# Global loads moved ahead of the global exchange in the written order of transfers

## The chip, the cores and the metric

The kernel runs on one core of one Trainium2 chip. Time is the device time of one execution in microseconds (us). Engines are named as in the profile: PE is TensorE, DVE VectorE, ACT ScalarE, POOL GpSimd, SP SyncE; SPq is the instruction queue of SP, from which nearly all transfers are issued.

## The reference

For 8 batches of 8 heads, sequences of 512 local and 32 global tokens with 64 elements a head: local tokens attend to the 32 global keys and to a band of 32 keys to either side; global tokens attend to everything. The result, as 4608 rows of 512, goes through a feed-forward network (FFN) with a leaky activation.

```python
s_g = scale * np.matmul(q_g, k_all.transpose(0, 1, 3, 2))
out_g = np.matmul(sm(s_g), v_all)
s_ll = np.where(mask, scale * np.matmul(q_l, k_l.transpose(0, 1, 3, 2)), -1000000000.0)
s_l = np.concatenate([s_lg, s_ll], axis=-1)
out_l = np.matmul(sm(s_l), np.concatenate([v_g, v_l], axis=2))
...
h = x @ w_in
g = np.maximum(h, 0.0) + alpha * np.minimum(h, 0.0)
return (g @ w_out).astype(np.float32)
```

## The kernel before

**FFN steps.** The FFN works on nine groups of tokens (eight batches of 512 local tokens, one of the 256 global tokens), each over 16 blocks of 128 hidden units: 144 steps. Step t computes the hidden block (`f1`, 12 matmuls into `h_ps`), lets ACT, DVE and POOL bend and split it (`g`, `gh`, `gl`), and two steps later adds it to the output (`f2`, 12 matmuls into `o0` to `o3`). One step of 512 tokens is some 5.5 us of matmuls.

**Attention between them.** The attention of later batches is put between the FFN steps. Local work goes by pairs of heads, 32 of them (`P`), one pair every four steps; such four steps are called a round here. Its transfers:

- `load_v` (two transfers, `vw`) and `load_qk` (one, `qk`) bring values, and queries with keys. From the fifth pair on each has a single buffer in SBUF, so the load for the next pair comes after the matmuls of this one.
- `local_scores` (`s_ps` from `qk`) and softmax; then `local_exchange` turns the weights round: DVE transposes 32 by 32 blocks (`pb`), two transfers write them to DRAM, eight read them back in another order (`pt`).
- `local_values` (`o_ps` from `vw` and `pt`), and `local_weights` with an exchange of the result: one transfer out (`xb`), four back (`x_raw`).

Global work goes by two pairs at a time, 16 tasks (`k`), three in every four rounds. `load_gn` brings queries and keys (two transfers, `gn`), `load_vg` values (two, `vg`); `global_scores` computes `g_ps` and its softmax, which ACT writes beside the keys; `global_transposes` is the global exchange: DVE transposes (`sgb`), one transfer out, four back into `sgt_sb`; `global_values` (`go` from `vg` and `sgt_sb`) and `global_outputs` follow with the next task's step. `gn` has one buffer, so task k+1's keys come after task k's scores. `vg` takes two buffers of a ring of three.

**Order.** The start, up to step 18, follows a list of words written by hand (`ORDER`); the word G0 is `global_scores(0)`. After it, a table `at` holds what attention work is done in which step and at which of its places (`pre`, `mid` after `f1`, `post` after the first half of `f2`); `plan` appends to it. Matmuls and the transfers issued by SP stay in the written order; the order on ACT and DVE in that part is the planner's, with a head start for attention work.

Local work of pair P is at step u = 4 (P - 4): values and the next pair's scores with their exchanges at u `post`, `load_v` and `load_qk` at u + 1 `post`. Global tasks stand between, at the steps u of the list `step` (18, 22, 26, 34, ...): scores at u `mid`, exchange at u + 1 `mid`. So in the written order of transfers a round with a global task reads `xb`, `x_raw` x4, `pb` x2, `pt` x8, `vw` x2, `qk`, `sgb`, `sgt_sb` x4, `vg` x2, `gn` x2. At the first step after each batch's end the four stores of results (`out` from `ost`) stand behind `qk`.

SP takes its queue in order: a transfer that waits for its data holds all behind it.

Of the kernel before, what the change touches and what calls it, by code (L numbers as in the profile page):

```python
# [17 lines left out]
NB, NH, SL, SG, D = 8, 8, 512, 32, 64  # L18
# [4 lines left out]
NPR = NB * NPAIR  # L23
# [61 lines left out]
def longformer_ffn(ctx: ExitStack, tc: tile.TileContext, qk, vs, gn, vg, w, alpha, out):  # L85
# [24 lines left out]
    def matmul(*a, **k):  # L110
        return tc.keep_in_program_order(nc.tensor.matmul(*a, **k))  # L111
# [4 lines left out]
    def stage(name, dtype=F32):  # L116
        return work.tile([128, 512], dtype, tag="st", name=name, bufs=NST)

    def small(name, n=4):
        return work.tile([128, n], F32, tag=name, name=name, bufs=4)  # L120
# [7 lines left out]
    def bank(tag, name):  # L128
        return psum.tile([128, 512], F32, tag=tag, name=name, bufs=2 if tag in "hs" else 1)
# [24 lines left out]
    def keep_warm(ps, n, add=False):  # L154
        for _ in range(n):
            matmul(ps, idle[:, 0:128], idle, start=not add, stop=not add)
# [3 lines left out]
    def wide(name, dtype=F32):  # L160
        return work.tile([128, 1024], dtype, tag="dec", name=name, bufs=3)
# [102 lines left out]
    def local_exps(P, heads=(0, 1)):  # L264
        if 0 in heads:
            z_of[P] = small("z", 8)
        for h in heads:
            src, mn, scale = ps_of.pop((P, h))
            p = pr_of[P, h] = stage("p") if P < NRAW else pr_of[P, h]
            for i in range(4):  # L270
                k = 2 * i + h
                act.activation(p[:, 128 * i : 128 * i + 128], src[:, i], AF.Exp, bias=mn[:, i : i + 1], scale=scale, accum_out=z_of[P][:, k : k + 1])
        if 1 in heads:
            rz_of[P] = small("rz", 8)
            act.activation(rz_of[P], z_of.pop(P), AF.Copy, bias=1e-9)
# [14 lines left out]
    def give(src, name):  # L290
        blk = stage(name)
        vec.transpose(blk.rearrange("k (b c n) -> k c b n", b=4, c=4), src.rearrange("q (c b n) -> q c b n", c=4, b=4))
        spread = dram.tile([128, 4, 128], F32, tag=name, name=name, bufs=2)
        dma.dma_start(spread, blk.rearrange("k (b n) -> k b n", b=4))
        return spread

    def take(put, spread):
        for b in range(4):
            dma.dma_start(put[32 * b : 32 * b + 32].rearrange("k (w n) -> k w n", w=4), spread[:, b].rearrange("(w k) n -> k w n", w=4))

    def local_exchange(P, heads=(0, 1)):
        dma.on = True
        for h in heads:
            ps_of[P, h] = give(pr_of.pop((P, h)), "pb")
        if 1 in heads:
            for h in range(2):
                pt_of[P, h] = stage("pt")
                take(pt_of[P, h], ps_of.pop((P, h)))
# [52 lines left out]
    def load_gn(k):  # L361
        if not big:
            big.append(wpool.tile([128, 2048], F32, tag="w", name="gn"))
        for e in range(2):
            gns[2 * k + e] = big[0][:, 576 * e : 576 * e + 576]
            dma.dma_start(gns[2 * k + e], gn[2 * k + e])

    def load_vg(k):
        for P in (2 * k, 2 * k + 1):
            vgs[P] = wide("vg")[:, 0:640].rearrange("k (y d) -> k y d", y=5)  # L370
            dma.dma_start(vgs[P], vg[P])
# [6 lines left out]
    def global_scores(k):  # L378
        ss = gps.pop(k)
        for r, c0, n in ((0, 32, 288), (1, 320, 256)):  # L380
            for e in range(2):
                t = gns[2 * k + e]
                for h in range(2):
                    hs, q0 = slice(64 * h, 64 * h + 64), 64 * r + 32 * e
                    matmul(ss[h][q0 : q0 + 32, 0:n], t[hs, 0:32], t[hs, c0 : c0 + n], start=True, stop=True)
        for e in range(2):
            del gns[2 * k + e]
        m, z = small("gm", 4), small("gz", 16)
        sg_sb = sgs[k] = big[0][:, 1152:1728].rearrange("q (h n) -> q h n", h=2)
        for h in range(2):  # L390
            vec.tensor_reduce(m[:, h : h + 1], ss[h][:, 0:288], axis=AX.X, op=ALU.max)
        vec.tensor_scalar(m[:, 2:4], m[:, 0:2], -0.125, None, op0=ALU.mult)
        vec.tensor_copy(m[0:64, 0:2], m[64:128, 2:4])
        vec.tensor_tensor(m[0:64, 2:4], m[0:64, 2:4], m[0:64, 0:2], op=ALU.min)
        vec.tensor_copy(m[64:128, 2:4], m[0:64, 2:4])
        for h in range(2):
            act.activation(sg_sb[:, h], ss[h][:, 0:288], AF.Exp, bias=m[:, 2 + h : 3 + h], scale=0.125, accum_out=z[:, h : h + 1])
        vec.tensor_copy(z[0:64, 2:4], z[64:128, 0:2])
        vec.scalar_tensor_tensor(z[0:64, 2:4], z[0:64, 2:4], 1e-9, z[0:64, 0:2], op0=ALU.add, op1=ALU.add)
        vec.reciprocal(z[0:64, 2:4], z[0:64, 2:4])  # L400
        vec.tensor_copy(z[64:128, 2:3], z[0:64, 3:4])
        gz[k] = z
# [79 lines left out]
    def f2(T, part, warm=0):  # L482
        G, f = divmod(T, NF)
        kind, b = GROUPS[G]
        n = SL if kind == "l" else NB * SG
        if f == 0 and part == 0:
            obs[G] = [bank(f"o{m}", f"o{m}") for m in range(NC)]
        o = obs[G]
        if T == NT - 1:
            if part:  # L490
                last(T)
            return
        g2 = (gh_of, gl_of)[part][T]
        keep_warm(o[0], warm, f > 0 or part > 0)
        for m in range(NC):
            ms = slice(128 * m, 128 * m + 128)
            if part == 0:
                matmul(o[m][:, 0:n], wts[f, 1][:, 0, ms], g2[:, 0:n], start=(f == 0), stop=False)
                matmul(o[m][:, 0:n], wts[f, 1][:, 1, ms], g2[:, 0:n], start=False, stop=False)
            else:  # L500
                matmul(o[m][:, 0:n], wts[f, 1][:, 0, ms], g2[:, 0:n], start=False, stop=(f == NF - 1))
        if part == 0:
            return
        del gh_of[T], gl_of[T]
        if f == NF - 1:
            col = b * SL if kind == "l" else NB * SL
            for m in range(NC):
                st = stage("ost")
                copy("ad"[m % 2], st[:, 0:n], o[m][:, 0:n])
                dma.dma_start(out[m, :, col : col + n], st[:, 0:n])  # L510

    def last(T):
        G, f = divmod(T, NF)
        n, o = width(T), obs[G]
        for m in range(NC):
            ms = slice(128 * m, 128 * m + 128)
            for j, g2 in ((0, gh_of), (1, gh_of), (0, gl_of)):
                matmul(o[m][:, 0:n], wts[f, 1][:, j, ms], g2[T][:, 0:n], start=False, stop=(g2 is gl_of))
            st = stage("ost")
            copy("ad"[m % 2], st[:, 0:n], o[m][:, 0:n])  # L520
            (dma, act)[m % 2].dma_start(out[m, :, NB * SL : NB * SL + n], st[:, 0:n])
# [3 lines left out]
    def plan(t, where, fn, P):  # L525
        at.setdefault((t, where), []).append((fn, P))
# [13 lines left out]
    for P in range(NRAW + 1, NPR):  # L540
        u = 4 * (P - NPAIR)
# [7 lines left out]
    for k in range(NPR // 2):  # L549
        u, v = step[k], step[k + 1]  # L550
        if k:
            plan(u - 1, "post", global_fill, k)
            plan(u, "mid", global_scores, k)
        plan(u + 1, "mid", global_transposes, k)
        plan(u + 1, "mid", load_vg, k)
        if k + 1 < NPR // 2:
            plan(u + 1, "mid", load_gn, k + 1)
        at.setdefault((v, "mid"), []).insert(0, (global_values, k))
        at.setdefault((v + 1, "mid"), []).insert(0, (global_outputs, k))

# [43 lines left out]
    def first_join(f):  # L604
        join(f)
        if f + 6 < NF:
            load_weights(f + 6)

    on_tensor = {"S": first_scores, "T": local_transposes, "V": first_values, "X": local_outputs, "F": first_f1, "A": lambda T, n: f2(T, 0, n), "B": lambda T, n: f2(T, 1, n)}
    others = {"R": local_maxima, "E": local_exps, "C": local_copies, "N": local_weights, "x": round_x, "y": rest_x, "D": local_exchange, "p": lambda P: local_exps(P, (0,)), "q": lambda P: local_exps(P, (1,)), "d": lambda P: local_exchange(P, (0,)), "e": lambda P: local_exchange(P, (1,)), "f": global_fill, "G": global_scores, "h": take_high, "k": take_low, "s": shift, "j": first_join, "u": upper, "l": lower, "r": leak, "g": bend, "H": round_g, "L": rest_g}  # L610
    for word in ORDER.split():
        word, _, warm = word.partition("*")
        if word[0] in on_tensor:
# [5 lines left out]
    for t in range(NF + 3, NT + LAG):  # L619
        with boost(t + HPU):  # L620
            attention(t, "pre")
        G, f = divmod(t + 1, NF)
# [69 lines left out]
```

## Time and profile before

| what | value |
|---|---|
| median of 3 runs | 915.15 us (913.53 to 915.3) |
| the profiled execution, time | 915.33 us |
| the profiled execution, span from first to last instruction | 913.6 us |
| PE busy | 882.2 us (97%) |
| DVE, ACT, POOL busy | 458.5, 377.9, 162.9 us |
| transfers of SP's queue | 147.11 MB |
| mean granted TensorE clock | 0.991 |

The rows of the profile shown below give times from the span's start. A group's row has its busy time, the mean of one instruction in ns, and after the second bar the idle time of the engine ahead of it with what ended most of it. A row of stretches has the stretch, its length, then busy time and count for PE, PE's weight loads, DVE, ACT and POOL, the granted clock, the busy share of the DMA engines and the GB/s they moved.

### The profile page before, as it was taken

The page shows a single profiled execution, that of the slowest core. Times are in us where ns is not written, and L with a number is a line of the kernel's source. Part 1 is how long each engine was busy: PE and PEld are TensorE (multiplying, and loading weights), DVE is VectorE, ACT ScalarE, POOL GpSimd, SP SyncE. Part 2 cuts the span into 40 slices and gives each one's busy share as a digit, 9 for nine tenths or more (in the row PEclk, how much of TensorE's full clock was granted, in tenths as well). Part 3 has the DMA queues.
Part 4 walks back from the last instruction along what each step waited for, and adds up shares of the span by engine and source line. Part 5 has one row for each costly group of instructions (what it writes and reads, how often), then busy time and mean ns, then how long its engine had stood idle before and what let it go on. Part 6 is the DMA issues. An engine that isn't in the chain of part 4 may idle for free.

```text
span 913.6 us, 21261 instructions
## 1 busy us (share of the span) xinstructions
PE 882.2 (97%) x8600; PEld 712.0 (78%) x8608; DVE 458.5 (50%) x983; ACT 377.9 (41%) x1030; POOL 162.9 (18%) x157
## 2 busy tenths in 40 slices
PE   7889999999989999999999999999999999999998
PEld 4668787777868778787777778777777888888898
DVE  6899997555435554555355544554445333111211
ACT  6787784334433324433343234433333333222322
POOL 3000000221111222121121221122122212222222
PEclk9999999999989999999999999999999999999999
DMA  9994233756456655655657565556656530100010
GB/s 335 396 358 169 83 119 97 232 175 197 159 164 223 198 175 187 201 176 175 189 172 233 169 202 177 163 201 197 188 176 206 161 116 24 47 1 1 1 48 24
DMA packets 151474, 148.73 MB, mean 163 GB/s; under 512 B 10576, under 2 KB 121680, under 8 KB 149328
## 3 DMA queue, kind: packets, MB, share of 16 engines
q1 hardware_dynamic: 151088, 147.11, 49.3%
q8 instruction: 68, 1.11, 0.5%
q14 instruction: 30, 0.25, 0.1%
q10 hardware_dynamic: 288, 0.26, 0.1%
HBM read 115.35 MB, written 31.98 MB: 161 GB/s over the span
## 4 chain that ended last, share of the span: by engine, by line
PE 73%; DMA 14%; SPq 6%; DVE 4%; issue 2%; ACT 1%; DVEq 0%; ACTq 0%
PE o L111 33%; PE h_ps L111 32%; DMA qk<-in_qk_dram 8%; SPq L78 6%; PE s_ps L111 4%; DMA xb<-xb 3%; PE o_ps L111 2%; DVE wt L78 2%; DMA pb<-pb 2%; PE go L111 1%; PE g_ps L111 1%; DMA ws<-in_w_dram 1%; DMA sgb<-sgb 1%; PE pt L114 0%; DVE xl L78 0%
## 5 line engine op out<-in xcount | busy, mean ns | idle before, releaser
L111 PE MATMUL h_ps<-xh,wt 128*128 128x512 f32 (+1 forms) x1152 | 340.8, 379 | 0.0
L479 POOL TENSOR_TENSOR gl<-g,gh 128x512 fp32r<-128x512 f32 (+1 forms) x128 | 155.8, 1217 | 744.2 <-ACT gh L78 562.8
L111 PE MATMUL o<-gh,wt 128*128 128x512 f32 (+1 forms) x1152 | 274.3, 380 | 0.0
L111 PEld LDWEIGHTS h_ps<-xh,wt 128*128 128x128 f32 x1152 | 212.8, 189 | 41.6 <-issue 0.6
L111 PEld LDWEIGHTS o<-gh,wt 128*128 128x128 f32 x1152 | 207.0, 188 | 46.1 <-ACT og_sb L78 6.6
L78 DVE SCALAR_TENSOR_TENSOR g<-g,beta_sb,h_ps 128x512 f32<-128x512 f32 (+1 forms) x144 | 103.0, 716 | 271.2 <-ACT g L78 270.5
L111 PE MATMUL h_ps<-xl,wt 128*128 128x512 f32 (+1 forms) x576 | 217.8, 378 | 0.0
L78 ACT ACTIVATE g<-h_ps 128x512 f32<-128x512 f32 (+1 forms) x144 | 82.0, 571 | 231.0 <-PE h_ps L111 225.4
L111 PE MATMUL o<-gl,wt 128*128 128x512 f32 (+1 forms) x576 | 152.6, 386 | 0.2 <-DVE gl L78 0.2
L78 ACT CAST gh<-g 128x512 fp32r<-128x512 f32 (+1 forms) x144 | 85.7, 597 | 104.2 <-DVE g L78 101.5
L111 PEld LDWEIGHTS h_ps<-xl,wt 128*128 128x128 f32 x576 | 108.7, 189 | 20.2
L111 PEld LDWEIGHTS o<-gl,wt 128*128 128x128 f32 x576 | 103.8, 190 | 23.8 <-issue 4.5
L78 ACT ACTIVATE p<-p,mn 128x128 f32<-128x128 f32 x192 | 74.4, 390 | 110.5 <-DVE mn L78 85.2
L78 DVE STREAM_TRANSPOSE pb<-p 128x512 f32<-128x512 f32 x48 | 34.0, 710 | 44.1 <-ACT p L78 39.1
L111 PE MATMUL s_ps<-qk 64*32 64x128 f32 x2048 | 39.9, 288 | 12.9 <-DMA qk<-in_qk_dram 11.0
L111 PEld LDWEIGHTS s_ps<-qk 64*32 64x32 f32 x2048 | 30.6, 110 | 20.3 <-issue 15.7
L111 PEld LDWEIGHTS o_ps<-vw,pt 128*32 128x32 f32 x2048 | 30.9, 111 | 18.6 <-DVE g L78 7.0
L78 DVE TENSOR_TENSOR xq<-o_ps,rz 128x512 f32<-128x512 f32 x32 | 22.1, 691 | 43.2 <-PE o_ps L111 42.5
L111 PE MATMUL o_ps<-vw,pt 128*32 128x64 f32 x2048 | 37.3, 223 | 6.0 <-DMA vw<-in_vs_dram 3.0
L78 ACT ACTIVATION_READ_ACCUMULATOR p<-p,mn 128x1 f32 x192 | 36.0, 187 | 0.0
L78 DVE SCALAR_TENSOR_TENSOR p<-s_ps,mask 128x512 f32<-128x512 f32 x48 | 30.7, 675 | 9.4 <-PE s_ps L111 9.4
L78 ACT ACTIVATE gn<-g_ps,gm 128x288 f32<-128x288 f32 x32 | 15.7, 496 | 40.1 <-DVE gm L78 40.1
(76 smaller groups left out, 530.1 us busy)
## 6 DMA issues: line engine op xcount, KB each, us to landing
vw<-in_vs_dram SPq DMA_DIRECT2D x64, 512.0 KB, 5.0
qk<-in_qk_dram SPq DMA_DIRECT2D x32, 672.0 KB, 6.9
ws<-in_w_dram SPq DMA_DIRECT2D x16, 1024.0 KB, 9.0
pb<-pb SPq DMA_DIRECT2D x48, 256.0 KB, 2.2
pt<-pb SPq DMA_DIRECT2D x192, 64.0 KB, 1.9
vg<-in_vg_dram SPq DMA_DIRECT2D x32, 320.0 KB, 3.7
gn<-in_gn_dram SPq DMA_DIRECT2D x32, 288.0 KB, 5.0
out_dram<-ost SPq DMA_DIRECT2D x32, 256.0 KB, 5.9
```

Source lines behind the costliest of these rows:

```text
L78: ins = call(*a, **k)
L111: return tc.keep_in_program_order(nc.tensor.matmul(*a, **k))
L479: (vec if T < NF else nc.gpsimd).tensor_tensor(gl[:, 0:n], gs.pop(T)[:, 0:n], gh_of[T][:, 0:n].bitcast(F32), op=ALU.subtract)
```

## The change

The loads of values and of the next task's keys are put at u `post`, right behind the task's scores in the table, instead of at u + 1 `mid`, behind the exchange. In the order of transfers a global round then reads `vw` x2, `qk`, `vg` x2, `gn` x2, `sgb`, `sgt_sb` x4. For the first task they are called right behind G0 in the hand-written list. Number, sizes and buffers of the transfers stay.

```diff
         plan(u + 1, "mid", global_transposes, k)
-        plan(u + 1, "mid", load_vg, k)
-        if k + 1 < NPR // 2:
-            plan(u + 1, "mid", load_gn, k + 1)
+        if k:
+            plan(u, "post", load_vg, k)
+        if 0 < k < NPR // 2 - 1:
+            plan(u, "post", load_gn, k + 1)
...
+    def first_global(k):
+        global_scores(k)
+        load_vg(k)
+        load_gn(k + 1)
...
-    others = {... "G": global_scores, ...}
+    others = {... "G": first_global, ...}
```

More of the change, by code (lines that the diff above doesn't have):

```diff
@@ L607, in first_join @@
             load_weights(f + 6)
+    def first_global(k):
+        global_scores(k)
+        load_vg(k)
+        load_gn(k + 1)
     on_tensor = {"S": first_scores, "T": local_transposes, "V": first_values, "X": local_outputs, "F": first_f1, "A": lambda T, n: f2(T, 0, n), "B": lambda T, n: f2(T, 1, n)}
-    others = {"R": local_maxima, "E": local_exps, "C": local_copies, "N": local_weights, "x": round_x, "y": rest_x, "D": local_exchange, "p": lambda P: local_exps(P, (0,)), "q": lambda P: local_exps(P, (1,)), "d": lambda P: local_exchange(P, (0,)), "e": lambda P: local_exchange(P, (1,)), "f": global_fill, "G": global_scores, "h": take_high, "k": take_low, "s": shift, "j": first_join, "u": upper, "l": lower, "r": leak, "g": bend, "H": round_g, "L": rest_g}
+    others = {"R": local_maxima, "E": local_exps, "C": local_copies, "N": local_weights, "x": round_x, "y": rest_x, "D": local_exchange, "p": lambda P: local_exps(P, (0,)), "q": lambda P: local_exps(P, (1,)), "d": lambda P: local_exchange(P, (0,)), "e": lambda P: local_exchange(P, (1,)), "f": global_fill, "G": first_global, "h": take_high, "k": take_low, "s": shift, "j": first_join, "u": upper, "l": lower, "r": leak, "g": bend, "H": round_g, "L": rest_g}
     for word in ORDER.split():
```

## The prediction

> **What bounds the kernel now.** I read the groups of instructions first, then the busy time by stretches, then the order of the Sync queue (SPq), which issues every transfer here, and last the sizes and landings of its transfers. The group row of the local score matmuls gives, after the bar, their busy time, the mean of one, and the idle time ahead of them with what ended it.
>
> ```profile
> L111 PE MATMUL s_ps<-qk 64*32 64x128 f32 x2048 | 39.9, 288 | 12.9 <-DMA qk<-in_qk_dram 11.0
> ```
>
> TensorE hardly ever idles in this kernel, and where it does in the main loop it waits for the queries and keys. The stretches below are the five batches in which both local and global attention run (length, then PE busy), and after them two short stretches.
>
> ```profile
> 176.00:270.00 94.00, 88.47 (x946) 70.90 (x945) 44.83 (x110) 35.67 (x111) 17.72 (x14) 0.96 0.55 174
> 270.00:376.00 106.00, 105.66 (x1135) 84.43 (x1135) 53.95 (x140) 40.92 (x123) 20.83 (x17) 1.00 0.59 188
> 376.00:480.00 104.00, 100.53 (x1017) 80.80 (x1019) 51.86 (x134) 39.15 (x120) 20.54 (x16) 0.98 0.59 187
> 480.00:585.00 105.00, 101.88 (x1104) 81.70 (x1096) 52.40 (x136) 40.38 (x122) 20.56 (x16) 1.00 0.60 190
> 585.00:690.00 105.00, 101.23 (x1048) 81.00 (x1044) 52.51 (x136) 39.44 (x122) 20.54 (x16) 1.00 0.60 189
> 258.40:265.20 6.80, 6.19 (x74) 4.97 (x75) 3.88 (x9) 2.18 (x11) 0.00 (x0) 0.50 0.18 59
> 442.70:446.10 3.40, 2.92 (x67) 2.37 (x68) 1.31 (x3) 0.00 (x0) 0.00 (x0) 0.50 0.13 39
> ```
>
> PE idles 5.53, 0.34, 3.47, 3.12 and 3.77 us in batches 1 to 5, 16.2 us in all. The two short rows follow the longest waits: there the granted clock is 0.50, so half of the busy time is lost besides, 6.19/2 = 3.1 and 2.92/2 = 1.5 us. All that a change of transfers can win is 16.2 + 4.6 = 20.8 us; the DMA engines are only 0.55 to 0.60 busy.
>
> Why the loads are late is seen in the order of the queue. Columns: start, length, instruction. This is a round of four FFN steps in which the queue runs behind; the last two rows are a lone exchange with nothing ahead of it.
>
> ```profile
> 646.27 0.52 SPq L78 DMA_DIRECT2D qk<-in_qk_dram  x1
> 646.89 0.50 SPq L78 DMA_DIRECT2D sgb<-sgb  x1
> 654.00 3.27 SPq L78 DMA_DIRECT2D sgt_sb<-sgb  x4
> 657.31 0.90 SPq L78 DMA_DIRECT2D vg<-in_vg_dram  x2
> 658.32 0.86 SPq L78 DMA_DIRECT2D gn<-in_gn_dram  x2
> 659.26 0.38 SPq L78 DMA_DIRECT2D xb<-xb  x1
> 664.09 1.75 SPq L78 DMA_DIRECT2D x_raw<-xb  x4
> ...
> 671.77 1.06 SPq L78 DMA_DIRECT2D vw<-in_vs_dram  x2
> 672.93 1.35 SPq L78 DMA_DIRECT2D qk<-in_qk_dram  x1
> 679.71 0.34 SPq L78 DMA_DIRECT2D xb<-xb  x1
> 681.76 2.09 SPq L78 DMA_DIRECT2D x_raw<-xb  x4
> ```
>
> The queue is a serial chain: sgb goes out, 7.11 us pass until its four readers (sgt_sb) may be issued, 3.31 us later the global loads start, after another 1.95 us xb goes out, and 4.83 us pass until x_raw may be issued; then the next queries are issued 8.84 us later. From qk to qk this is 26.66 us. xb pays 4.83 us because vg and gn were issued just ahead of it; alone it pays 2.05. Since each round's qk stands behind all of this, every round in which the chain is longer than PE's own round makes PE wait.
>
> **The change part by part.** It removes and adds no transfer. In each global round four issues (two vg, two gn; two vg alone in the last) move ahead of five (sgb and four sgt_sb) on the Sync queue, directly behind qk; for the first global task they come right behind its scores. They pass no other queue; POOL's has none of them. Each move is priced by the row sizes:
>
> ```profile
> vw<-in_vs_dram SPq DMA_DIRECT2D x64, 512.0 KB, 5.0
> qk<-in_qk_dram SPq DMA_DIRECT2D x32, 672.0 KB, 6.9
> ...
> vg<-in_vg_dram SPq DMA_DIRECT2D x32, 320.0 KB, 3.7
> gn<-in_gn_dram SPq DMA_DIRECT2D x32, 288.0 KB, 5.0
> out_dram<-ost SPq DMA_DIRECT2D x32, 256.0 KB, 5.9
> ```
>
> ```profile
> 672.93 6.31 DMA qk<-in_qk_dram
> ```
>
> The global loads are 2x320 + 2x288 = 1216 KB. Their time on the DMA engines, d, is the unknown of this change, since sgb will now stand behind them. My rate: two vw and one qk are 1696 KB; the chain row just above says qk landed 6.31 us after 672.93, which is 7.47 after the first vw was issued at 671.77; less the 2.05 us that a lone transfer needs, 1696 KB take 5.42 us, 313 KB/us, so d = 3.9 us. Upper end: xb landed 664.09 - 657.31 = 6.78 us after the first vg, less 2.05, 4.7 us. Lower end: the busiest of the 40 slices moves 396 GB/s, 3.1 us.
>
> ```profile
> GB/s 335 396 358 169 83 119 97 232 175 197 159 164 223 198 175 187 201 176 175 189 172 233 169 202 177 163 201 197 188 176 206 161 116 24 47 1 1 1 48 24
> ```
>
> I take 3.9, as it comes from loads of the same kind running back to back. The Trainium skill, DMA: Bandwidth & Descriptors, section Anatomy of one DMA, gives a fit of about 2.0 us plus bytes over 436 GB/s; by it d would be an estimated 2.9 us and each gain below 1 us larger. The rows show less than that rate, so I keep 3.9.
>
> (a) A round that runs behind. Saved: the 1.95 us of issue between sgt_sb and xb, since the loads are issued while vw and qk still move, and 4.83 - 2.05 = 2.78 us of xb's landing. Paid: d = 3.9 us on sgb's landing. Net 0.8 us earlier, by the ends of d between 0.0 and 1.6. I use 1.0, as any stall in issuing vg and gn goes off the chain too.
>
> (b) A round in which the queue waits for VectorE's sgb.
>
> ```profile
> 587.29 1.06 SPq L78 DMA_DIRECT2D vw<-in_vs_dram  x2
> ...
> 589.69 1.81 SPq L78 DMA_DIRECT2D out_dram<-ost  x4
> 597.54 0.33 SPq L78 DMA_DIRECT2D sgb<-sgb  x1
> 600.50 1.75 SPq L78 DMA_DIRECT2D sgt_sb<-sgb  x4
> ...
> 604.24 0.38 SPq L78 DMA_DIRECT2D xb<-xb  x1
> 609.76 1.77 SPq L78 DMA_DIRECT2D x_raw<-xb  x4
> ```
>
> The queue stands idle from 591.5 to 597.54; the loads fall into this hole. The engines then hold 1696 + 4x256 + 1216 = 3936 KB, 12.6 us at 313 KB/us, and sgb lands near 587.29 + 12.6 + 2.05 = 601.9 instead of 600.5: 1.4 us lost there. xb goes out no later than now (603.8 against 604.24) and lands in about 2.05 instead of 5.52 us. At most 3.5 us are won, at least 0 if the hole is used up; I take 2.0, nearer the middle since 3936 KB back to back is more than any row shows. The first round of each batch is of this kind.
>
> (c) What the loads put behind qk do to qk itself. With nothing behind it qk landed in 6.31 us; with the four result stores behind it, at 691.86, in
>
> ```profile
> DMA to landing us min/median/max: 7.8/7.8/7.8
> ```
>
> 1.5 us later; the median of all, most of which have sgb behind them, is 6.9 (its size row), 0.6 of it paid already. So the cost is between 0 and 0.9; I take 0.4. [...]
>
> (d) Covers. sgt_sb lands later by up to d. Its reader is the matmul of the next global values (go).
>
> ```profile
> 626.52 1.75 SPq L78 DMA_DIRECT2D sgt_sb<-sgb  x4
> ```
>
> ```profile
> 636.17 0.77 PE L111 MATMUL go<-vg,sgt_sb 128*32 128x64 f32 x40
> 636.87 0.69 PE L111 MATMUL g_ps<-gn 64*32 64x288 f32 x16
> ```
>
> sgt_sb's last issue ends at 628.27 and lands some 2 us later, so go has nearly 6 us of cover against d = 3.9 (at most 4.7): cost nothing, and 1 us for each us above 6. The new waits: vg's buffers wait for go, gn's for g_ps, done at 637.56 here, while the queue is past qk and comes to the loads only at 646.8; it is 9 us behind. Cost nothing; if the cover went, sgb and xb would stand behind the wait. VectorE's and ScalarE's order may be planned a little differently; no row prices it, so I put it between -1 and +1 us and take 0.
>
> **The sum.** Arrival of the loads in batches 2 to 5: 2.0 earlier from the first round, 1.0 more in each of the next two, 0.4 less by (c): 1.6, 2.6 and 3.6 us, against accumulated PE waits of at most 0.34, 3.47, 3.12 and 3.77 us at the batch's end. On paper their 10.7 us all but vanish. But the margins are a few tenths, and lengths of one issue scatter (qk 0.52 and 1.35, sgt_sb 1.75 and 3.27 above), so I leave a third: 7.1 us won. Batch 1 has no such hole at its start, so I count three rounds at 1.0 less 0.4, 2.6 of 5.53 us, of which two thirds are 1.7. The short half-clock stretch (1.5) goes with its wait; the long one (3.1) follows the wait that stays, and I leave it. Together 7.1 + 1.7 + 1.5 = 10.3 us. The profiled execution has a span of 913.6 and a time of 915.33 (0.18 above the median of the runs), so 915.3 - 10.3 = 905 us. This measurement can tell about 0.2%, 1.8 us, from no change.
>
> **Rivals.**
> All waits go. Holes and hidden stalls add up to more than I allow, batch 1 included: 915.3 - 20.8 = 894.5 us. For it: the paper sum above covers batches 2 to 5; against: batch 1's 5.53. The Trainium skill, TensorE: Matmul & The Clock Gate, section What's actually happening, ties the half clock to an idle window of about 3.4 us; the trace halves it after shorter, split waits, so I don't count on a wait under 3.4 us being safe.
> Only moved. With d at 4.7 a round behind gains 0.0 and the hole's gain is eaten by (c): within 1.8 us, about 915. For it: the bytes on the same engines are the same; against: xb's 5.52 in a round where the queue had idled.
> Slower, by qk itself. If 1216 KB behind qk slow it by the whole 1.5 us of (c) and rounds gain 0.0, the four batches that wait now wait 1.5 longer each: 915.3 + 6 = 921 us. It decides where the slowing exceeds the 2.0 of (b). For it: the 7.8 row; against: 0.6 of it is paid now.
> The loads don't go early. If the queue were held at vg or gn for PE, sgb would be no earlier and xb no faster: 915 us. Against: the 9 us in (d).
>
> **How the numbers follow.** Forecast 0.47 (its own range 899 to 911), all waits go 0.22, only moved 0.16, held 0.03, slower 0.12. Faster 0.69, within 0.2% 0.19, slower 0.12. The range 894 to 916.5 leaves out the slower case and the tails.
>
> **What will show it.** Right: x_raw follows xb by about 2 us in every round; sgt_sb follows sgb by 8 to 11 us where the queue has no hole; qk to qk under 26 us; PE idle under 2 us in batches 2 to 5; the clock at 0.50 once at most. Wrong: sgb's landing grows by more than 4.7, qk lands in 7.8 or more with PE still waiting for it, or go waits for sgt_sb.

## The result: 892.1 us, faster by 2.5%

The median of four runs is 892.12 us (890.18 to 893.7) against 915.22 before; the ratio is 0.9748, 95% interval 0.9723 to 0.9773. Forecast were 905 us with a range of 894 to 916.5: the direction was right, the size was more than twice the forecast, and even the rival in which all waits go, 894.5 us, fell short. The profiled execution took 892.45 us with a span of 890.7, which is 22.9 us less than the profiled execution before.

The group rows of the two attention matmuls in the profile after (after the last bar: idle time ahead of them):

```profile
L111 PE MATMUL s_ps<-qk 64*32 64x128 f32 x2048 | 37.2, 274 | 0.0
L111 PE MATMUL o_ps<-vw,pt 128*32 128x64 f32 x2048 | 36.5, 223 | 0.5 <-DVE pt L78 0.5
```

The 12.9 us that the scores stood idle are 0.0. Stretches of the kernel after, with the columns as before:

```profile
200.00:300.00 100.00, 100.00 (x1061) 80.37 (x1060) 52.91 (x136) 39.87 (x121) 20.59 (x16) 1.00 0.62 205
300.00:400.00 100.00, 100.00 (x1062) 80.33 (x1061) 52.88 (x136) 39.89 (x121) 20.60 (x16) 1.00 0.56 186
400.00:500.00 100.00, 100.00 (x1061) 80.37 (x1060) 53.02 (x136) 39.88 (x121) 19.62 (x16) 1.00 0.61 201
500.00:600.00 100.00, 100.00 (x1062) 80.33 (x1061) 52.29 (x135) 39.26 (x121) 20.25 (x16) 1.00 0.58 191
600.00:690.00 90.00, 90.00 (x968) 72.65 (x967) 46.52 (x110) 36.06 (x112) 18.01 (x14) 1.00 0.59 192
```

PE is busy without a break through the stretch in which it idled in five batches, and the granted clock is never below 1.00 there. What is left idle lies ahead of step 18 and in the tail. The order of the Sync queue in a round that runs behind:

```profile
194.07 1.06 SPq L78 DMA_DIRECT2D vw<-in_vs_dram  x2
195.23 1.42 SPq L78 DMA_DIRECT2D qk<-in_qk_dram  x1
196.69 0.96 SPq L78 DMA_DIRECT2D vg<-in_vg_dram  x2
197.75 0.85 SPq L78 DMA_DIRECT2D gn<-in_gn_dram  x2
198.69 0.38 SPq L78 DMA_DIRECT2D sgb<-sgb  x1
206.11 1.75 SPq L78 DMA_DIRECT2D sgt_sb<-sgb  x4
207.96 0.38 SPq L78 DMA_DIRECT2D xb<-xb  x1
210.04 1.73 SPq L78 DMA_DIRECT2D x_raw<-xb  x4
211.86 0.85 SPq L78 DMA_DIRECT2D pb<-pb  x2
214.01 4.31 SPq L78 DMA_DIRECT2D pt<-pb  x8
218.36 1.06 SPq L78 DMA_DIRECT2D vw<-in_vs_dram  x2
219.52 1.00 SPq L78 DMA_DIRECT2D qk<-in_qk_dram  x1
```

From vw to vw this round takes 24.29 us (218.36 - 194.07). xb may be read 2.08 us after it was issued, where it took 4.83 before, and it follows sgt_sb at once. The readers of sgb wait 7.42 us, less than the 8 to 11 that the prediction named as a sign. Over the rounds that run behind they wait 7.5 us on average, against 6.5 before; besides, sgb is issued 4.38 us after the first vw instead of 2.57, as four issues now stand ahead of it. x_raw followed xb within 2.6 us in 14 of the 16 global rounds, and after 4.50 us at the slowest.

I took the same four pieces of every round that runs behind (sgb issued over 0.4 us after VectorE had it ready), as means in us; "landed" is the end of the transfer:

| piece | before, 7 rounds | after, 4 rounds |
|---|---|---|
| first vw issued to sgb landed | 9.02 | 11.83 |
| sgb landed to xb issued | 4.82 | 1.88 |
| xb issued to xb landed | 5.10 | 2.19 |
| xb landed to next vw issued | 8.52 | 8.73 |
| whole round | 27.46 | 24.63 |

PE's own round, with no wait, takes 25.64 us where a global task is in it (scores to scores in nearly all such rounds of the kernel after) and 24.10 where there is none. So the chain before was 1.8 us too long, and is now 1.0 us short: of the 16 rounds with a global task only seven before, and four after, were behind at sgb, and after the change the queue catches up instead of losing more.

The order of instructions on DVE and ACT is the same in both kernels, so no planner's choice is in this difference. It is the same in the eight kernels below too.

### The profile page after: what moved, and what is told of

Its sections match the earlier page's. It is cut to its first block, busy times and chain, and to the rows that moved or that the text cites. A ratio compares the mean times of both kernels' runs of the same rounds, so it can differ in the third digit from the quotient of the medians.

```text
span 890.7 us, 21285 instructions
## 1 busy us (share of the span) xinstructions
PE 877.3 (98%) x8608; PEld 707.6 (79%) x8608; DVE 460.1 (52%) x983; ACT 377.3 (42%) x1030; POOL 163.0 (18%) x157
## 4 chain that ended last, share of the span: by engine, by line
PE 93%; DVE 3%; SPq 1%; DMA 1%; issue 1%; ACT 0%; DVEq 0%
PE o L111 42%; PE h_ps L111 41%; PE o_ps L111 4%; PE s_ps L111 3%; DVE wt L78 2%; SPq L78 1%; PE go L111 1%; DMA ws<-in_w_dram 1%; PE g_ps L111 1%; DVE xl L78 0%; PE pt L114 0%; ACT wt L78 0%; PE xt L114 0%; DVE g L78 0%; DVE mn L78 0%
## 5 line engine op out<-in xcount | busy, mean ns | idle before, releaser
L111 PE MATMUL h_ps<-xh,wt 128*128 128x512 f32 (+1 forms) x1152 | 339.9, 378 | 0.0
L111 PE MATMUL o<-gh,wt 128*128 128x512 f32 (+1 forms) x1152 | 274.3, 380 | 0.0
L111 PEld LDWEIGHTS h_ps<-xh,wt 128*128 128x128 f32 x1152 | 212.0, 188 | 41.3 <-issue 0.9
L111 PEld LDWEIGHTS o<-gh,wt 128*128 128x128 f32 x1152 | 207.0, 188 | 46.1 <-ACT og_sb L78 6.6
L111 PE MATMUL h_ps<-xl,wt 128*128 128x512 f32 (+1 forms) x576 | 217.5, 378 | 0.0
L111 PE MATMUL o<-gl,wt 128*128 128x512 f32 (+1 forms) x576 | 151.2, 383 | 0.2 <-DVE gl L78 0.2
L111 PEld LDWEIGHTS h_ps<-xl,wt 128*128 128x128 f32 x576 | 108.4, 188 | 20.4 <-DVE xl L78 0.3
L111 PEld LDWEIGHTS o<-gl,wt 128*128 128x128 f32 x576 | 102.9, 188 | 23.4 <-issue 4.2
L111 PEld LDWEIGHTS o_ps<-vw,pt 128*32 128x32 f32 x2048 | 31.0, 112 | 12.7 <-DVE g L78 7.4
L111 PE MATMUL s_ps<-qk 64*32 64x128 f32 x2048 | 37.2, 274 | 0.0
L111 PE MATMUL o_ps<-vw,pt 128*32 128x64 f32 x2048 | 36.5, 223 | 0.5 <-DVE pt L78 0.5
L111 PEld LDWEIGHTS s_ps<-qk 64*32 64x32 f32 x2048 | 28.5, 105 | 5.9 <-issue 2.5
```

## The experiments

Two theories stood at the start. Theory A: the Sync queue is one serial chain, PE waits when its round is longer than PE's, and each change to it counts by the time that it adds to that chain. Rival B: what counts is the hole of the first round of a batch, in which the queue waits for VectorE; there the loads cost nothing, while elsewhere they are only moved. The first four kernels were timed against the same runs of before (median 915.96 us), the other four against 914.33.

**The move in some rounds only.**

```diff
 # first_rounds: early = k % 3 == 0;  later_rounds: early = k % 3 != 0
-        if k:
-            plan(u, "post", load_vg, k)
-        if 0 < k < NPR // 2 - 1:
-            plan(u, "post", load_gn, k + 1)
+        early = ...
+        where = (u, "post") if early else (u + 1, "mid")
+        if k or not early:
+            plan(*where, load_vg, k)
+            if k < NPR // 2 - 1:
+                plan(*where, load_gn, k + 1)
```

This is against the changed kernel. In later_rounds the first task's loads are also back behind its exchange. Expected of first_rounds:

> Loads moved only for the first global task of each batch (k a multiple of 3); the others as before. Theory A (the Sync queue is a serial chain; every moved round shortens it, from some 27.4 us to under 25.6): the later rounds still run 27 us, the early start of some 3 us is used up by the end of the batch: 898 to 904 us, waits for qk of 0.5 to 1.5 us left in the last rounds of batches. Rival B (only the hole counts in which the queue waits for sgb; in rounds that run behind the move is a swap of equal sums): 892 to 894 us, as with all moved. Rival C (the hole is worth nothing): 912 us or more.

Measured: 901.11 us (895.22 to 905.38), ratio 0.9863, 0.9825 to 0.9901. Expected of later_rounds:

> Loads moved only for the second and third global task of each batch; the first as before. Theory A: the batch starts with its lag of some 2 us and loses it again: 894 to 900 us, a wait of under 1 us for qk in some rounds. Rival B: 908 to 915 us. Rival C: 892 to 894 us.

Measured: 895.69 us (892.07 to 897.68), ratio 0.9784, 0.9753 to 0.9814. Both fall where theory A put them; each half alone wins most of the whole, 14.9 and 20.3 of some 23 us. This fits theory A, by which a batch is saved either by a lead at its start or by rounds that catch up. Rival B fails on both, rival C on the first. The ten rounds of first_rounds whose loads were not moved took 26.6 us on average, where some 27 were expected, and are still longer than PE's 25.64. In first_rounds the waits that stay are at the ends of batches (waits of PE, total, times, longest; its profiled execution is the fastest of its runs, so its list is short):

```profile
PE s_ps L111 <- DMA qk<-in_qk_dram: 1.9, 2, 1.1
PE o_ps L111 <- DMA vw<-in_vs_dram: 1.2, 2, 0.9
```

In later_rounds ten rounds were behind at sgb and took 24.83 us on average, the same as after the whole change. One of its rounds was different: global values (go) waited 1.3 us,

```profile
PE go L111 <- DVE g L78: 1.3, 1, 1.3
```

in a round where sgb landed 9.38 us after its issue. The cover (d) of the prediction had not run out there: this go began at 317.42, and the last of its sgt_sb transfers had landed at 314.62, before the wait of 1.3 us began. The row names VectorE; why it was late there stays open.

**Half of the loads.** values_only moves `load_vg` alone, keys_only `load_gn` alone; the other stays behind the exchange.

```diff
 # values_only
         if k:
             plan(u, "post", load_vg, k)
-        if 0 < k < NPR // 2 - 1:
-            plan(u, "post", load_gn, k + 1)
+        if k < NPR // 2 - 1:
+            plan(u + 1, "mid", load_gn, k + 1)
...
     def first_global(k):
         global_scores(k)
         load_vg(k)
-        load_gn(k + 1)
```

> Only the global values (vg, 640 KB a task) are moved, the next task's keys (gn) stay behind the exchange. Theory A: about half of the bytes and of the issue time leave the stretch between sgt_sb and xb, the round is some 26 us: 895 to 903 us, xb lands in 3 to 3.5 us. Rival D (any load ahead of xb costs nearly the whole round trip, so that half a move wins little): 906 to 914 us, xb at 4 us or more.

Measured: 897.16 us (894.9 to 899.77), ratio 0.9805, 0.9776 to 0.9834.

> Only the next task's keys (gn, 576 KB) are moved, the values (vg) stay behind the exchange. Theory A: as with the values alone, 895 to 903 us, xb lands in 3 to 3.5 us. Rival D: 906 to 914 us.

Measured: 900.51 us (900.15 to 904.21), ratio 0.985, 0.9822 to 0.9877. Rounds behind took 25.58 (4 of them) and 25.89 us (8), between the 27.46 of the kernel before and the 24.63 of the changed one, so that they win 1.9 and 1.6 us of the 2.8. The order of a round of values_only, from qk to x_raw:

```profile
423.91 1.38 SPq L78 DMA_DIRECT2D qk<-in_qk_dram  x1
425.33 0.91 SPq L78 DMA_DIRECT2D vg<-in_vg_dram  x2
426.34 0.38 SPq L78 DMA_DIRECT2D sgb<-sgb  x1
433.06 1.75 SPq L78 DMA_DIRECT2D sgt_sb<-sgb  x4
434.91 0.85 SPq L78 DMA_DIRECT2D gn<-in_gn_dram  x2
435.85 0.38 SPq L78 DMA_DIRECT2D xb<-xb  x1
439.52 1.75 SPq L78 DMA_DIRECT2D x_raw<-xb  x4
```

xb lands in 3.67 us, between 2.08 and 4.83. In the rounds behind it landed in 4.10 (values) and 4.34 us (keys) on average. On this sign theory A missed, with its 3 to 3.5, and rival D, with 4 or more, was right: half of the loads ahead of xb cost it more than half of the delay. But the times are theory A's, not the 906 or more of D, since the length of the round has other parts besides. A round as long as PE's own, or a little longer, leaves small waits for qk: in the batches five of 4.3 us in all with the values, nine of 8.1 with the keys (the profiled executions are the fastest and the slowest of their runs).

**The same bytes, the chain made long again.** six_small adds to the changed kernel six transfers of 2 KB, in every global round, into columns that nobody reads.

```diff
 # spare: new columns of alpha's tile
...
 # global_transposes, behind the four reads into sgt_sb
+        for i in range(6):
+            dma.dma_start(spare[:, 4 * i : 4 * i + 4], alpha[:, 0:4])
```

> The changed kernel with six transfers of 2 KB each issued between sgt_sb and xb in every global round. Theory A: they lengthen the chain by 6 x 0.45 = 2.7 us of issue, from 24.6 to 27.3 us in a round that runs behind, as long as before the change: 908 to 918 us, with waits for qk and vw at the ends of batches. Rival F (the bytes ahead of xb are what counts): 12 KB are nothing, 890 to 895 us.

Measured: 923.23 us (922.04 to 927.62), ratio to before 1.0114, 1.0069 to 1.016: slower than before the change, above the upper end of what I expected. The rows show a round and its waits; L112 is the line that is L111 in the other kernels, and the last two rows are those of the kernel before.

```profile
206.05 1.75 SPq L78 DMA_DIRECT2D sgt_sb<-sgb  x4
207.85 2.81 SPq L78 DMA_DIRECT2D alpha_sb<-in_alpha_dram  x6
210.75 0.38 SPq L78 DMA_DIRECT2D xb<-xb  x1
212.83 1.75 SPq L78 DMA_DIRECT2D x_raw<-xb  x4
```

```profile
PE s_ps L112 <- DMA qk<-in_qk_dram: 10.9, 12, 1.5
PE o_ps L112 <- DMA vw<-in_vs_dram: 8.4, 8, 2.0
```

```profile
PE s_ps L111 <- DMA qk<-in_qk_dram: 11.0, 12, 1.5
PE o_ps L111 <- DMA vw<-in_vs_dram: 3.0, 5, 0.9
```

xb still lands in 2.08 us, and 12 KB are no load for the engines; yet a round that runs behind is 27.59 us long, as before the change (27.46), and the waits are back, 10.9 us for qk, 9.2 of them in the batches (11.0 before), and 8.4 for vw (3.0 before). This is what tells the length of the chain from the bytes: rival F is out. Eleven rounds were behind here, seven before, and in the batches the clock stood at 0.50 for 17.1 us, where it was 10.2 before; both fit the larger loss.

**The loads between sgb and its readers.** The queue sends sgb first and issues the loads while it waits for sgb to land.

```diff
         dma.dma_start(spread, blk.rearrange("k (b n) -> k b n", b=4))
+        load_vg(k)
+        if k + 1 < NPR // 2:
+            load_gn(k + 1)
         for b in range(4):
...
-        plan(u + 1, "mid", load_vg, k)
-        if k + 1 < NPR // 2:
-            plan(u + 1, "mid", load_gn, k + 1)
```

This is against the kernel before.

> The loads stand behind the first transfer of the global exchange (sgb) and ahead of its four reads (sgt_sb). Theory A (the length of the Sync queue's chain against TensorE's round): sgb again lands some 9 us after the values' load (12 with the loads ahead), the loads' issue lies in the wait for that landing, a round that runs behind takes 22 to 24 us; as no wait for loads is left in the changed kernel there is nothing to win: 890 to 894 us. Rival E (what counts is that the loads stand ahead of sgb): waits of the kernel before come back, 900 us or more.

Measured: 891.28 us (890.35 to 893.44), ratio 0.9759, 0.972 to 0.9799, the same as the changed kernel.

```profile
625.65 0.34 SPq L78 DMA_DIRECT2D sgb<-sgb  x1
626.05 1.92 SPq L78 DMA_DIRECT2D vg<-in_vg_dram  x2
628.06 0.86 SPq L78 DMA_DIRECT2D gn<-in_gn_dram  x2
629.01 1.81 SPq L78 DMA_DIRECT2D sgt_sb<-sgb  x4
633.34 0.34 SPq L78 DMA_DIRECT2D xb<-xb  x1
636.51 1.73 SPq L78 DMA_DIRECT2D x_raw<-xb  x4
```

sgb's readers follow 3.36 us after it, and from then on the queue waits for VectorE's xb: it is behind at sgb in no round, so the 22 to 24 us that were expected of such a round can't be read. In the eleven global rounds without result stores sgb lands 9.16 us after the first vw on average, as expected, against 11.99 in the changed kernel and 8.88 before. The chain has more to spare, but there is nothing left to win with it. That the loads stand ahead of sgb isn't needed (rival E); that they don't stand between the exchange and xb is.

**No global loads behind the first task.** The loads of the later tasks are left out, and these compute on the first one's data.

> The changed kernel with the global loads of the first task alone; all later tasks compute on its data, so their output is another. Theory A: in the changed kernel the loads are hidden whole, TensorE sets the time: 889 to 893 us, the same as with the loads within 0.2%. Rival G (the loads still cost time by their bytes): 880 to 887 us.

Measured: 893.52 us (891.96 to 895.6), ratio 0.9782, 0.9741 to 0.9823. This is a little above what I expected, though its runs overlap those of the changed kernel. 18.7 MB less (15 tasks of 1216 KB) make it no faster: the loads are hidden whole in the changed kernel (rival G is out).

**The first task's loads back at their place.**

```diff
     def first_global(k):
         global_scores(k)
-        load_vg(k)
-        load_gn(k + 1)
```

with its two loads planned behind its exchange again.

> The changed kernel with the first task's loads back behind its exchange. Theory A: one round of the first batch is 1 to 3 us longer; the other rounds of that batch make up for it or leave a wait under 1 us: 891 to 895 us. Rival H (the first batch, where the kernel before lost most, is saved by the first task's loads): 898 us or more, with waits for qk near 200 to 255 us.

Measured: 890.93 us (890.69 to 892.2), ratio 0.9756, 0.9711 to 0.98. This is a hair under what theory A gave, and far from rival H. The part of the change in the hand-written list does nothing that can be measured; batch 1, which had lost most, is saved by its later rounds. One wait is left:

```profile
PE s_ps L111 <- DMA qk<-in_qk_dram: 0.3, 1, 0.3
```

## Why the prediction was right in kind and wrong in size

**What bounds the kernel** was read rightly: a serial queue, whose lateness PE feels at qk and vw. Lengthening it by issue alone brought the waits back (six_small), and shortening it, by moving loads ahead of sgb or behind it, took them away.

**Step (a), a round that runs behind**, is the step that failed, by its size: 1.0 us was put down as its gain (0.0 to 1.6), 2.8 us were measured (27.46 to 24.63). Its parts:

- xb's landing was right, 2.91 us saved against 2.78.
- Between sgb's landing and xb's issue not 1.95 but 2.94 us went: besides the loads' issue, stalls in issuing sgt_sb, vg and gn that stood on the chain (sgt_sb's four issues took 2.51 us on average in the rounds behind before, 1.75 after).
- The cost to sgb, d, was put at 3.9 us with ends of 3.1 and 4.7; sgb landed 2.8 us later (11.83 - 9.02), and 3.3 in later_rounds. Of the 2.8, 1.8 is sgb's later issue and 1.0 its longer way to landing.
- The last piece, from xb's landing to the next vw, grew by 0.2.

One reason why d was too large is in the trace: my rate of 313 KB/us counts the slow start of vw and qk. The engines moved 104 GB/s in 672.8:673.8, but 346 to 394 in each of the three us from 674.8. By that rate d would be an estimated 3.2 to 3.6 us; why sgb lost less still stays open. The Trainium skill, DMA: Bandwidth & Descriptors, section Anatomy of one DMA, states its fit for transfers that GpSimd issues; its slope gave an estimated 2.9 us for these, which SP issues, and the 2.8 measured here is near it.

**Step (b), the hole**, put at 2.0 us in the first round of a batch, was near: over the five rounds with a hole, xb landed 2.35 us earlier, counted from sgb's issue (9.25 against 11.60 us on average). In one such round after,

```profile
567.13 2.35 SPq L78 DMA_DIRECT2D vw<-in_vs_dram  x2
569.59 1.26 SPq L78 DMA_DIRECT2D qk<-in_qk_dram  x1
570.94 1.82 SPq L78 DMA_DIRECT2D out_dram<-ost  x4
572.81 1.35 SPq L78 DMA_DIRECT2D vg<-in_vg_dram  x2
574.25 3.19 SPq L78 DMA_DIRECT2D gn<-in_gn_dram  x2
578.58 0.33 SPq L78 DMA_DIRECT2D sgb<-sgb  x1
583.44 1.93 SPq L78 DMA_DIRECT2D sgt_sb<-sgb  x4
585.48 0.38 SPq L78 DMA_DIRECT2D xb<-xb  x1
587.90 2.39 SPq L78 DMA_DIRECT2D x_raw<-xb  x4
```

sgb's readers come 4.86 us after it instead of 2.96, 1.9 us lost where 1.4 were forecast, and xb lands in 2.42 instead of 5.52. That first_rounds, which moves these loads and the first task's, won 14.9 us, some 3 us for each of five batches, is more than this term: a lead at the start also spares later waits, and the clock was never at 0.50 in the batches of its profiled execution.

**Step (c)** put 0.4 us on qk, which the runs don't show in the rounds that run behind. In the eleven global rounds without result stores qk landed in 6.86 us on average with the global loads behind it, and in 7.05 in the same rounds before, in seven of which sgb stood right behind it. With nothing behind it qk took 6.35 us (six loads of the kernel after): what stands behind it costs it some 0.5 us, but the kernel before had paid that already. In the five rounds with stores it was 7.72 against 7.44. The slowest of the eleven, issued at 622.47:

```profile
DMA to landing us min/median/max: 7.6/7.6/7.6
```

Two loads with stores and global loads behind them took longer, 8.27 and 8.23 us; PE waited for neither.

**Step (d)** held in the changed kernel: no wait of go is in its trace. sgt_sb landed at least 3.3 us before go began, where it was 5.8 before. The queue waited for go, which frees vg's buffers, for 0.7 us in two waits.

**The sum** failed at the third that I left standing, and at batch 1. Both came from adding up leads that (a) had made too small and setting them against past waits. With 2.8 in the place of 1.0 the same sum gives batch 1 a lead of 8.0 us (3 x 2.8 less 0.4) against waits of 5.53, and nothing is left to hold back. The right comparison was one of lengths: as soon as a round that runs behind is shorter than 25.64 us, lateness shrinks from round to round, and no batch needs a hole at its start. With (a) at its lower end of d, 27.46 less 1.6 gives 25.9, beside the edge; with what was measured it is past it, and all 16.2 us go with the 4.6 of half clock.

**The bound of 20.8 us** was too low by 1.6: the stretch with attention became 22.4 us shorter, and 0.5 came ahead of step 18. A part of each wait stands in the trace as busy time. Before, at one of them:

```profile
650.40 0.43 PE L111 MATMUL o_ps<-vw,pt 128*32 128x64 f32 x16
651.11 0.88 PE L111 MATMUL o_ps<-vw,pt 128*32 128x64 f32 x48 [0.28 <-DMA vw<-in_vs_dram]
653.45 1.15 PE L111 MATMUL s_ps<-qk 64*32 64x128 f32 x64 [1.46 <-DMA qk<-in_qk_dram]
```

and the same matmuls after:

```profile
631.37 1.10 PE L111 MATMUL o_ps<-vw,pt 128*32 128x64 f32 x64
632.40 1.16 PE L111 MATMUL s_ps<-qk 64*32 64x128 f32 x64
```

The 64 matmuls of values are shown busy for 0.43 + 0.88 = 1.31 us with the wait and 1.10 without, as the profile models the ends of matmuls. Rounds with waits were longer than PE's own round by more than the idle time shown: by 0.07 us where qk alone was late (six rounds), by 0.28 where vw was late too (three). The two pairs of rounds round the half-clock stretches were 3.3 and 1.7 us longer than their idle time, where 3.1 and 1.5 were put down; how much of that is the clock and how much hidden wait isn't separated. Added up this is the 1.6.

Of the rivals, "all waits go" came true, which had 0.22; its estimate of 894.5 missed by the hidden part. "Only moved" and "slower, by qk itself" were priced with d at 4.7, which no kernel showed on average.

## What to carry to other kernels

Where one queue issues everything in order, write down its round as a chain (issue times, landings that something waits for) and compare its length with the round of the engine that sets the time: a chain 1.8 us too long in 27 cost 22 us here, and 1.0 us of spare took all of it away. A load that nobody waits for soon belongs where the queue waits anyway, not ahead of a transfer whose landing the queue itself waits for: ahead of xb the loads cost 2.9 us of its landing, ahead of sgb 2.8, and between sgb and its readers next to nothing (9.16 us from vw to sgb's landing against 8.88 before). At its shortest, issuing a transfer took 0.33 us for 2 KB and 0.52 for 672 KB, and on such a chain issue time is as dear as bytes.

## What the runs showed of the hardware that was not expected

- 1216 KB queued directly behind other loads delayed the landing of the transfer behind them by 2.8 to 3.3 us, less than the 3.9 that the rate of vw and qk, start included, had given.
- Six transfers of 2 KB took 2.81 us to issue and turned a gain of 2.5% into a loss of 1.1%.
- In the kernel before the clock went to 0.50 at 442.71 us, after 3.41 us in which PE was busy for 1.69 us; no wait there was longer than 1.47 us. Waits of 0.28 and 1.46 us near 652 us were not followed by a lower clock.
- PE busy time is no measure of waits to a tenth of a us: some 0.2 us of a wait was shown as busy.
